# Second MoE of a chained kernel: where its second weights are split, and how a block's activations are split beside the block before

## The chip, the cores and the metric

One core of a Trainium2 chip runs the whole program in one launch. The metric is device time in microseconds (us): the kernel before took a median of 1038.61 us in 3 runs (1037.12 to 1039.48). The profile is of one further execution.

The core's engines run their own instruction queues in order and wait for each other by semaphores: TensorE (PE in the profile, its weight loads PEld) multiplies, VectorE (DVE) and GpSimd (POOL) do element-wise arithmetic, ScalarE (ACT) copies and applies functions, and SyncE (SP) issues the DMAs.

## The reference

All tensors are float; the MoE weights come as float64, and the kernel converts them to float32 itself ("wide" in the code).

```
x = attention(q, k, v, f)            # 4 x 8 heads, 576 tokens, 64 wide
x = x as 2304 tokens x 512
h = x @ moe_w_in                     # 512 -> 2048
g = h * clip(h + 3, 0, 6) / 6
x = g @ moe_w_out                    # 2048 -> 512
h = x @ moe2_w_in                    # the second MoE: 512 -> 2048
g = max(h, 0) + log1p(exp(-|h|))
out = g @ moe2_w_out                 # 2048 -> 512
```

## The kernel before, in words

The program is recorded as a list of operations, each with the engines that may do it, its planned cost, the data that it reads and writes, and a due time `at`. `Work.order` then simulates the engines and at each turn takes the operation that can start first, or, among those ready at once, the one with the smallest `at`; what comes out is one fixed order for each engine. An operation with two ways (`either`: VectorE or GpSimd) goes to the one that would end first by the planned costs, with 600 ns in GpSimd's favour (`pv`).

Every product in float32 precision is made of three matmuls on split operands: a high half (a copy in the type fp32r, made by ScalarE) and a low half (the operand less its high half, made by VectorE or GpSimd). So every weight and every activation that is multiplied needs one ScalarE copy and one subtraction.

**The first MoE** (lines 1278 to 1388) runs over five blocks of tokens, four of 512 and one of 256. The last two blocks run together, unit by unit (`NB - 2` and `NB - 1` in the code): 16 slices of the hidden width, for each of which both blocks have a first product (line 1290), the activation (lines 1330, 1332), its split (lines 1310, 1311, 1313) and a second product (line 1353). They stand at about 500 to 636 us of the span. In the same time the second MoE's first weights are loaded in float64 (line 1001), converted on VectorE and ScalarE (lines 1017 to 1023), combined (line 1100) and split (lines 1129, 1132) into the tiles that the first MoE's weights leave free.

**The second MoE** uses a Strassen scheme with 7 products in place of 8 (`SEVEN`). A unit is a pair `p` of slices, 8 units in all. For each unit four sums of the weight quarters are formed (line 1100) and seven factors split.
- *Stage A* (`step_a`, line 1406) is the first matrix with the softplus: 4 blocks `t` of 576 tokens, 8 steps `p` each, 42 matmuls a step. ScalarE copies four products of a step (line 1421), VectorE adds three (line 1424), and lines 1449, 1451 and 1452 make the softplus. The order of products in a step is `CHAIN`; the accumulators of a product that is added to can be used again only when the copy or the add is done.
- `factors_x(t)` prepares a block's activations: it loads them from x2_dram (line 1197), forms four differences (line 1212) and splits seven factors (lines 1206, 1207), into the tile XO for even blocks and MX and SB for odd ones. In the kernel before it is recorded at the start of block `t - 1`, with due times 4 us apart.
- `weights2_out(p)` prepares the second matrix of unit `p`: it loads the unit's two slices, converted earlier, from wf_dram (line 1086) into staging tiles (GT and rBL, or st), forms four sums (line 1100), splits seven factors (lines 1129, 1132) into four pairs of small buffers (`piece`) in SB, rBW, MX and PC, and stores each half to wo_dram (line 1161). In the kernel before it is recorded at every third step of stage A.
- *Stage B* (`step_b`, line 1507) is the second matrix; it loads the units back from wo_dram (line 1168) and prepares the activations of g (lines 1472 to 1490).

## Time and profile before

| | |
|---|---|
| three runs, median | 1038.61 us (1037.12 to 1039.48) |
| profiled execution, its own time | 1037.48 us |
| its span | 1035.7 us |
| TensorE busy | 985.4 us, 95% |
| VectorE, ScalarE, GpSimd busy | 835.5, 599.1, 281.7 us |
| granted TensorE clock, mean | 0.993 |
| first MoE's last blocks | about 500 to 636 us |
| stage A, blocks 0 to 3 | from 636.1, 690.9, 744.8 and 797.8 us |
| stage B | from about 843 us to the end |

Two views matter: how long each engine is busy in a stretch, and, for the engine that idles, what ended its idle time. The busy share over the whole span says little here, since the stages have different limits.

### The profile page before, as it was taken

How to read it: one execution, taken by the hardware profiler on the slowest of the kernel's cores; microseconds unless marked ns; L12 is line 12 of the kernel's file. 1: busy time of each engine (PE TensorE's matmuls, PEld its weight loads, DVE VectorE, ACT ScalarE, POOL GpSimd, SP SyncE). 2: the span in 40 equal slices, each digit the busy share in tenths (PEclk: the TensorE clock that was granted, in tenths of full speed). 3: DMA queues.
4: the chain of work that ended last, by engine and by line, in shares of the span. 5: the costliest groups of instructions: out<-in, count | busy, mean ns of one | idle time of the engine just before them, and what ended most of it. 6: DMA issues, size and time to landing. Idle time of an engine off the chain costs nothing.

```text
span 1035.7 us, 17877 instructions
## 1 busy us (share of the span) xinstructions
PE 985.4 (95%) x6116; PEld 853.1 (82%) x6116; DVE 835.5 (81%) x1653; ACT 599.1 (58%) x1309; POOL 281.7 (27%) x273
## 2 busy tenths in 40 slices
PE   8999998989999999999999999898989999999998
PEld 6666677768788888888788888797979999999997
DVE  8789979998998669986865656989796768888885
ACT  6898766877676556664443335656655544443342
POOL 2221231230000000000311211756560307454442
PEclk9999999999999999999999999999999999999999
DMA  6675553445553235412612114695963994445342
GB/s 140 161 155 141 134 148 94 119 142 147 130 153 95 59 114 149 113 43 78 195 44 65 58 41 156 203 307 197 323 228 127 344 373 157 123 124 153 113 126 77
DMA packets 192771, 151.50 MB, mean 146 GB/s; under 512 B 108988, under 2 KB 166492, under 8 KB 191784
## 3 DMA queue, kind: packets, MB, share of 16 engines
q1 hardware_dynamic: 192680, 150.36, 48.6%
q8 instruction: 48, 0.79, 0.3%
q14 instruction: 43, 0.35, 0.1%
HBM read 98.10 MB, written 52.21 MB: 145 GB/s over the span
## 4 chain that ended last, share of the span: by engine, by line
PE 63%; DVE 21%; issue 5%; DMA 4%; ACT 3%; POOL 2%; SPq 1%; DVEq 0%; ACTq 0%; POOLq 0%
PE bank L1507 15%; PE bank L1353 14%; PE bank L1290 14%; PE bank L1406 8%; PE bank L685 5%; PE bank L846 4%; PE bank L776 4%; DVE st L1020 2%; DVE st L1023 1%; DVE p L701 1%; DVE MX L1313 1%; DVE GT L1332 1%; DVE rBW L1449 1%; DVE KB L632 1%; SPq L535 1%
## 5 line engine op out<-in xcount | busy, mean ns | idle before, releaser
L1290 PE MATMUL bank<-MX,W 128*128 128x512 f32 x768 | 224.1, 405 | 1.7 <-DVE MX L886 1.0
L1353 PE MATMUL bank<-MX,W 128*128 128x512 f32 (+1 forms) x688 | 188.5, 382 | 3.7 <-DVE MX L1313 3.7
L1290 PEld LDWEIGHTS bank<-MX,W 128*128 128x128 f32 x768 | 133.6, 190 | 24.2 <-DVE MX L886 1.3
L1353 PEld LDWEIGHTS bank<-MX,W 128*128 128x128 f32 x688 | 121.3, 189 | 25.5 <-DVE MX L1313 4.3
L1507 PE MATMUL bank<-rW,rW 128*128 128x256 f32 x1134 | 138.7, 283 | 1.7 <-POOL rW L1132 0.9
L1507 PEld LDWEIGHTS bank<-rW,rW 128*128 128x128 f32 x1134 | 136.9, 191 | 2.6 <-POOL rW L1132 1.1
L1406 PE MATMUL bank<-XO,rW 128*128 128x288 f32 x672 | 97.2, 302 | 13.0 <-DVE rBW L1424 6.5
L1406 PEld LDWEIGHTS bank<-XO,rW 128*128 128x128 f32 x672 | 92.0, 191 | 17.6 <-DVE rBW L1424 8.2
L710 ACT ACTIVATE p<-p,stats 64x64 f32<-64x64 f32 (+4 forms) x130 | 72.3, 557 | 33.4 <-DVE stats L701 32.5
L1486 ACT ACTIVATE rW<-st 128x512 fp32r<-128x512 f32 (+1 forms) x72 | 36.9, 518 | 77.1 <-PE bank L1507 43.5
L1406 PE MATMUL bank<-MX,rW 128*128 128x288 f32 x480 | 71.1, 299 | 7.4 <-DVE HY L1424 4.5
L1036 POOL TENSOR_TENSOR W<-st,W 128x512 fp32r<-128x512 f32 x24 | 34.0, 1418 | 162.3 <-ACT W L1035 111.5
L1406 PEld LDWEIGHTS bank<-MX,rW 128*128 128x128 f32 x480 | 65.6, 188 | 10.0 <-DVE HY L1424 5.9
L1330 ACT ACTIVATE GT<-bank,three 128x512 f32<-128x512 f32 x80 | 51.1, 643 | 31.0 <-PE bank L1290 15.1
L581 POOL TENSOR_TENSOR V<-vr,V 128x640 fp32r<-128x640 f32 x10 | 17.1, 1715 | 189.8 <-ACT V L577 189.8
L776 PE MATMUL bank<-ident,p 128*128 128x128 f32 x390 | 58.7, 276 | 8.7 <-DVE xs L861 4.4
L776 PEld LDWEIGHTS bank<-ident,p 128*128 128x128 f32 x390 | 46.3, 141 | 24.8 <-DVE xs L861 3.9
L1313 DVE TENSOR_TENSOR MX<-GT,MX 128x512 fp32r<-128x512 f32 (+1 forms) x69 | 49.5, 720 | 21.1 <-ACT MX L1310 20.2
L811 ACT ACTIVATE pth<-bank 128x320 fp32r<-128x320 f32 (+2 forms) x100 | 42.5, 433 | 34.5 <-PE bank L776 25.7
L1490 POOL TENSOR_TENSOR rW<-st,rW 128x256 fp32r<-128x256 f32 (+1 forms) x35 | 40.9, 1173 | 73.2 <-ACT rW L1486 58.8
L701 DVE CUSTOM_DVE_ANT_0 p<-bank,bar 64x64 f32<-64x64 f32 (+4 forms) x130 | 52.1, 421 | 9.8 <-PE bank L685 9.0
L1332 DVE SCALAR_TENSOR_TENSOR GT<-GT,bank 128x512 f32<-128x512 f32 x80 | 49.9, 628 | 8.1 <-ACT GT L1330 7.5
(241 smaller groups left out, 2130.8 us busy)
## 6 DMA issues: line engine op xcount, KB each, us to landing
st<-g_dram SPq DMA_DIRECT2D x36, 512.0 KB
st<-in_moe_w_out_dram SPq DMA_DIRECT2D x32, 512.0 KB
st<-in_moe_w_in_dram SPq DMA_DIRECT2D x26, 512.0 KB
g_dram<-HY SPq DMA_DIRECT2D x16, 576.0 KB
g_dram<-rBW SPq DMA_DIRECT2D x16, 576.0 KB
rW<-wo_dram SPq DMA_DIRECT2D x5, 1792.0 KB
wo_dram<-SB SPq DMA_DIRECT2D x42, 128.0 KB
wo_dram<-rBW SPq DMA_DIRECT2D x42, 128.0 KB
```

Of the source, the lines that this page charges most:

```text
L685: nc.tensor.matmul(acc[:r, o:o + c - a], qs[:, q0:q0 + r], ks[:, a:c], start=(n == 0 and ti == todo[-1][0]), stop=(n == len(ops) - 1), ski ...
L701: nc.vector.tensor_tensor_reduce(out=T["P"][par][ti][:r, a:c], in0=bank[bk.i][:r, o:o + c - a], in1=bar[:r, b0:b0 + c - a], op0=ALU.add, o ...
L710: nc.scalar.activation(out=pt, in_=pt, func=ACTF.Exp, scale=-1.0, bias=sv[:r, 0, ti:ti + 1], accum_out=sv[:r, 1, ti:ti + 1],)
L776: nc.tensor.transpose(acc[:, p0:p0 + P], T["P"][par][ti][:, k0:k0 + P], ident)
L811: nc.scalar.activation(out=place("PTH", j, ks, a, c), in_=src(), func=ACTF.Copy)
L1290: nc.tensor.matmul(bank[bk.i][:, 0:n], w[:, c], x[:, c, 0:n], start=(c == 0 and p == 0), stop=(c == NC - 1 and p == 2))
L1313: op(("dve", dve(n), lambda: nc.vector.tensor_tensor(t(glt), g, t(ght).bitcast(F32), op=ALU.subtract)), r=[("g", i), ("gh", i3)], w=[("gl" ...
L1330: op(("act", act(n, True, 1), lambda: nc.scalar.activation(out=g, in_=bank[bk.i][:, 0:n], func=ACTF.Relu, bias=three)), r=["three"], banks ...
L1332: op(("dve", dve(n), lambda: nc.vector.scalar_tensor_tensor(out=g, in0=g, scalar=6.0, in1=bank[bk.i][:, 0:n], op0=ALU.min, op1=ALU.mult)), ...
L1353: nc.tensor.matmul(bank[b][:, o:o + n], w[:, c * P:(c + 1) * P], x, start=(ft == 0 and p == 0 and o == 0), stop=(ft == NF - 1 and p == 2), ...
L1406: nc.tensor.matmul(bank[bks[b].i][:, 0:HA], wa[u][:, c], xa[v][:, c], start=(nm in ("P1", "P2", "P5") and c == 0 and y == 0), stop=(c == 1 ...
L1507: nc.tensor.matmul(bank[bks[b].i][:, o * 256:(o + 1) * 256], ga[u], wa[v], start=(p == 0 and o == 0 and y == 0), stop=(p == NPR - 1 and y ...
```

## The change

`weights2_out` moves from stage A into the first MoE's last two blocks: it is recorded there for units 0 to 6, with due times beside those of the first weights. Its loads go to the tile XO (four slices' room, used by turns), its sums to XT, and its split factors to the rest of XO: 11 pieces, each with both halves, stored by one DMA of 256 KB where two of 128 KB stood. XO and XT are those that `factors_x(0)` fills, which now comes behind all of this. The tile PC goes.

`factors_x(t + 1)` is recorded after step 6 of block `t`, with due times 5 us apart, and each of its differences and ScalarE copies gets one more dependency ("pace"): the i-th waits for product P6 of step i of block `t`.

```diff
     def weights2(o, p, at, parts, i0):
...
+        own = i0 >= 8
+
+        def raw(i):
+            return BIG["XO"][:, (i - 8) * NC * P:(i - 7) * NC * P].bitcast(F32)
...
         for z in range(2):
             i, ft = i0 + z, 2 * p + z
-            if (o, ft) in late2:
+            if not own and (o, ft) in late2:
                 raw_weights(i, 1, o, ft, at, True)
...
             def load(i=i, ft=ft):
-                dst = words(i)[:, 0]
+                dst = raw(i) if own else words(i)[:, 0]
                 if wide:
                     nc.sync.dma_start(out=dst, in_=wf_dram[o, ft])
...
-            dma(load, 4 * P * NC * P, w=[("stage", i), ("up", i)] + [("o", i, 0), ("o", i, 1)] * (i < 2), r=["m2"] * (i in (2, 3)) + [("wf", o, ft)],
+            dma(load, 4 * P * NC * P, w=[("stage", i), ("up", i)] + [("o", i, 0), ("o", i, 1)] * (i < 2), r=["m2"] * (i in (2, 3) or own) + [("wf", o, ft)],
                 at=at - 15, name="loadwf")
...
         def x(i, e, j, n=1):
+            if own:
+                return (BIG["XT"][:, i * 2 * h:] if e else raw(i0 + i))[:, j * h:(j + n) * h]
             return words(i0 + i)[:, e, j * h:(j + n) * h]
...
-        s0, s1, u0, u1 = ((x, i0 + i) for x in ("stage", "up") for i in range(2))
+        s0, s1, u0, u1 = ((x, 8 + i if own and x == "up" else i0 + i) for x in ("stage", "up") for i in range(2))
...
-            rd = [("stage", i0 + i), ("up", i0 + i)]
+            rd = [(s0, s1)[i], (u0, u1)[i]]
...
+    NPC = (7 * XW - 4 * NC * P) // (4 * P)
+
     def piece(i):
-
-        t, a = ((BIG["SB"], 2 * XW + i * 2 * P) if i < 3 else (BIG["rBW"], 2 * XW + (i - 3) * 2 * P) if i < 6 else
-                (MX, 5 * XW) if i == 6 else (BIG["PC"], 0))
-        return t[:, a:a + 2 * P]
+        return BIG["XO"][:, 4 * NC * P + i * 4 * P:][:, 0:4 * P].rearrange("p (s f) -> p s f", s=2)
...
         for z in range(7):
-            i = pieces[0] % 4
+            i = pieces[0] % NPC
             pieces[0] += 1
...
             def store(z=z, i=i):
-                for s in range(2):
-                    dma(lambda s=s: nc.sync.dma_start(out=wo_dram[p][:, (s * 7 + z) * 2 * P:(s * 7 + z + 1) * 2 * P], in_=piece(2 * i + s).bitcast(F32)), 8 * P * P,
-                        r=[("piece", i)], w=[("wo", p, z, s)], at=at, name="storewo")
-
-            parts.append((z, z + 1, lambda s, i=i: piece(2 * i + s).bitcast(F32R), [("piece", i)], store))
+                dma(lambda: nc.sync.dma_start(out=wo_dram[p].rearrange("p (s z f) -> p s z f", s=2, z=7)[:, :, z], in_=piece(i).bitcast(F32)), 16 * P * P,
+                    r=[("piece", i)], w=[("wo", p, z)], at=at, name="storewo")
+
+            parts.append((z, z + 1, lambda s, i=i: piece(i)[:, s], [("piece", i)], store))
         weights2(1, p, at, parts, i0)
...
         dma(lambda: nc.sync.dma_start(out=unit2_w(p).rearrange("p s z f -> p (s z f)").bitcast(F32), in_=wo_dram[p]), 4 * P * UW,
-            r=[("wo", p, z, s) for z in range(7) for s in range(2)], w=[("unit2", p)], at=at, name="loadwo")
+            r=[("wo", p, z) for z in range(7)], w=[("unit2", p)], at=at, name="loadwo")
...
     def factors_x(t, at, step):
 
         z = t % 2
+
+        def pace(x):
+            return [("pace", t - 1, x)] if t else []
...
-        def split(f, src, key, at):
-            op(("act", act(n, False), lambda: nc.scalar.activation(out=xf(z, f, 0), in_=src(), func=ACTF.Copy)), r=[key], w=[("xf", z, f)], at=at, name="xfh")
+        def split(f, src, key, at, x):
+            op(("act", act(n, False), lambda: nc.scalar.activation(out=xf(z, f, 0), in_=src(), func=ACTF.Copy)), r=[key] + pace(x), w=[("xf", z, f)], at=at, name="xfh")
             op(either(n, lambda e: e.tensor_tensor(xf(z, f, 1), src(), xf(z, f, 0).bitcast(F32), op=ALU.subtract)), r=[key], w=[("xf", z, f)], at=at, name="xfl")
 
...
             key = [("xt", y) if isinstance(y, int) else ("xf", z, y) for y in (a, b)]
-            op(either(n, go), r=key + ["m2"], w=[("xt", d)], at=at + step * i, name="x" + f)
-            split(f, lambda d=d: sm(d), ("xt", d), at + step * (i + 0.5))
+            op(either(n, go), r=key + ["m2"] + pace(i), w=[("xt", d)], at=at + step * i, name="x" + f)
+            split(f, lambda d=d: sm(d), ("xt", d), at + step * (i + 0.5), i)
         for i, f in enumerate(("B11", "B21", "B22")):
-            split(f, lambda f=f: raw(f), "m2", at + step * (4 + i))
+            split(f, lambda f=f: raw(f), "m2", at + step * (4 + i), 4 + i)
...
-        for nm, n in (("XO", 7 * XW), ("SB", 2 * NC * tokens(LAST_B) + 2 * TB), ("PC", 2 * P)):
+        for nm, n in (("XO", 7 * XW), ("SB", 2 * NC * tokens(LAST_B) + 2 * TB)):
...
-            op(("pe", 6 * (0.447 * HA + 2.5), go), r=[("unit", p), ("xf", z, f)], w=[bks[b]], banks=[bks[b]], at=at, name=nm, seq="s" if nm in ("P1", "P2", "P5") else None)
+            op(("pe", 6 * (0.447 * HA + 2.5), go), r=[("unit", p), ("xf", z, f)], w=[bks[b]] + [("pace", t, p)] * (nm == "P6"), banks=[bks[b]], at=at, name=nm, seq="s" if nm in ("P1", "P2", "P5") else None)
...
     for p in range(NPR):
         freed(of_pair(p), [("unit", p)], lambda p=p: again(p, UW, F32R, ("U", p)))
         weights2_in(0, p, moe_at(NB - 2, 2 * p + 2) + 14, 2 if p in (1, 3, 5) else 0)
+        if p < NPR - 1:
+            weights2_out(p, moe_at(NB - 2, 2 * p + 1) + 14, 8 + p % 2 * 2)
         if p == NPR - 2:
...
+    freed([("stage", 8 + i) for i in range(4)] + [("piece", i) for i in range(NPC)], [("xf", 0, f) for f in AT[2]])
+    freed([("up", 8), ("up", 9)], [("xt", 0), ("xt", 1)])
     factors_x(0, M2_0 - 45, 4.0)
...
-    freed([(x, c) for x in "XY" for c in range(NC)] + [(x, i) for x in ("gh", "gl") for i in range(3)], [("xf", 1, f) for f in AT[2]] + [("piece", i) for i in range(4)])
+    freed([(x, c) for x in "XY" for c in range(NC)] + [(x, i) for x in ("gh", "gl") for i in range(3)], [("xf", 1, f) for f in AT[2]])
     for t in range(NTA):
         for p in range(NPR):
-            if p == 0 and t + 1 < NTA:
-                factors_x(t + 1, ma_at(t, 1), 4.0)
-            if p % 3 == 0 and (t * NPR + p) // 3 < NPR - 1:
-                weights2_out((t * NPR + p) // 3, ma_at(t, p, 3) + 4, 4 * (1 - (t * NPR + p) // 3 % 2))
             step_a(t, p)
+            if p == NPR - 2 and t + 1 < NTA:
+                factors_x(t + 1, ma_at(t, 1), 5.0)
             if t == NTA - 1:
                 if p < 2:
```

In the six pieces below names are the program's tiles: XO and XT as above, W and rW weights, HY and rBW the sums of stage A, st and HY staging tiles. Line numbers of the changed kernel are up to 9 higher from line 1074 on.

GpSimd at the start of the first MoE's last blocks, before: the first weights' sums (line 1100), and `factors_x(0)` (lines 1212, 1207).

```order
L1272 TENSOR_TENSOR SB<-SB 128x256 x3
L1100 TENSOR_TENSOR HY<-HY 128x256 x3
L1212 TENSOR_TENSOR XT<-XO,XT 128x576
L1207 TENSOR_TENSOR XO<-XT,XO 128x576
L1212 TENSOR_TENSOR XT<-XO,XT 128x576
L1100 TENSOR_TENSOR st_170<-st_171 128x256
L1100 TENSOR_TENSOR st_170<-st_170 128x256
```

The three rows of 576 columns are the ones that leave this place.

The same place after the change.

```order
L1281 TENSOR_TENSOR SB<-SB 128x256
L1107 TENSOR_TENSOR XT<-XO 128x256 x2
L1107 TENSOR_TENSOR XT<-XO,XT 128x256 x2
L1139 TENSOR_TENSOR XO<-XT,XO 128x256
L1139 TENSOR_TENSOR XO<-XO 128x256 x3
L1139 TENSOR_TENSOR XO<-XT,XO 128x256 x2
L1107 TENSOR_TENSOR XT<-XO,XT 128x256
L1107 TENSOR_TENSOR XT<-XO 128x256
L1107 TENSOR_TENSOR HY<-HY 128x256 x2
L1139 TENSOR_TENSOR XO<-XO 128x256 x2
L1139 TENSOR_TENSOR XO<-XT,XO 128x256
```

Behind the split of the last block's activations (line 1272, now 1281), nine rows of `weights2_out` stand where three of `factors_x(0)` stood.

VectorE in stage A, block 0, before: stage A's own lines 1424, 1449 and 1452, `factors_x(1)` (lines 1212, 1207), a weight sum (line 1100) and the last unit's first weights (line 1132).

```order
L1132 TENSOR_TENSOR rW_5665<-st_170,rW_5665 128x1024
L1424 TENSOR_TENSOR rBW<-rBW,bank_69 128x288
L1100 TENSOR_TENSOR rBL<-rBL,GT 128x256
L1449 TENSOR_SCALAR rBW<-rBW 128x2x288
L1132 TENSOR_TENSOR rW_5665<-st_171,rW_5665 128x512
L1212 TENSOR_TENSOR XT<-MX,XT 128x576
L1452 SCALAR_TENSOR_TENSOR rBW<-rBW 128x2x288
L1424 TENSOR_TENSOR rBW<-rBW,bank_69 128x288
L1132 TENSOR_TENSOR rW_5665<-st_171,rW_5665 128x256
L1207 TENSOR_TENSOR SB<-XT,SB 128x576
L1449 TENSOR_SCALAR rBW<-rBW 128x576
L1424 TENSOR_TENSOR HY<-HY,bank_72 128x288
```

Between two of line 1424 stand up to three operations that are not stage A's own.

VectorE in the same block after the change, some steps further: lines 1433, 1458 and 1461 are stage A's own, line 1216 is `factors_x(1)`.

```order
L1433 TENSOR_TENSOR HY<-HY,bank_71 128x288
L1458 TENSOR_SCALAR HY<-HY 128x576
L1461 SCALAR_TENSOR_TENSOR HY<-HY 128x2x288
L1433 TENSOR_TENSOR rBW<-rBW,bank_70 128x288
L1461 SCALAR_TENSOR_TENSOR HY<-HY 128x576
L1433 TENSOR_TENSOR rBW<-rBW,bank_72 128x288
L1458 TENSOR_SCALAR rBW<-rBW 128x2x288
L1216 TENSOR_TENSOR MX<-XT,MX 128x576
L1461 SCALAR_TENSOR_TENSOR rBW<-rBW 128x2x288
L1433 TENSOR_TENSOR rBW<-rBW,bank_72 128x288
L1458 TENSOR_SCALAR rBW<-rBW 128x576
L1216 TENSOR_TENSOR MX<-MX 128x576
```

Between two of line 1433 stands at most one factor operation; the weight sums are gone.

SP in the first MoE's last blocks, before: stores of block 2's result (line 1385), loads of the activations (line 1197) and of the first weights (line 1001).

```order
L1385 DMA x2_dram2_83<-st0_170 128x512 x2
L1385 DMA x2_dram2_83<-st1_171 128x512
L1197 DMA XO_4513<-x2_dram1_82 128x2x64
L1197 DMA XT_4516<-x2_dram1_82 128x2x64
L1001 DMA st0_170<-in_moe2_w_in_dram 128x4x256
L1385 DMA x2_dram2_83<-st1_171 128x512
L1197 DMA XT_4516<-x2_dram1_82 128x2x160
L1001 DMA st1_171<-in_moe2_w_in_dram 128x4x256
```

The loads of the first weights stand behind block 2's stores and the loads of `factors_x(0)`, which have moved back.

SP at the same place after the change (line 1394 the same stores, line 1166 the stores to wo_dram, line 1001 the first weights).

```order
L1394 DMA x2_dram2_83<-st0_170 128x512 x2
L1394 DMA x2_dram2_83<-st1_171 128x512
L1166 DMA wo_dram0_137<-XO_4513 256x1x256 x4
L1001 DMA st0_170<-in_moe2_w_in_dram 128x4x256
L1166 DMA wo_dram0_137<-XO_4513 256x1x256 x3
L1394 DMA x2_dram2_83<-st1_171 128x512
L1166 DMA wo_dram1_138<-XO_4513 256x1x256 x6
L1001 DMA st1_171<-in_moe2_w_in_dram 128x4x256
```

The loads of the first weights now stand behind stores that wait for the second weights' splits.

## Rows read from the trace of the kernel before

**Rows 1.** the page's first part: busy us (share of the span) xinstructions, by engine.

```profile
PE 985.4 (95%) x6116; PEld 853.1 (82%) x6116; DVE 835.5 (81%) x1653; ACT 599.1 (58%) x1309; POOL 281.7 (27%) x273
```

**Rows 2.** by stretch: us; PE, PEld, DVE, ACT, POOL busy (instructions); clock; DMA share; GB/s.

```profile
520.00:636.00 116.00, 116.00 (x665) 101.13 (x666) 69.11 (x122) 45.93 (x85) 19.43 (x25) 1.00 0.18 55
636.00:691.00 55.00, 47.53 (x328) 45.26 (x327) 50.58 (x76) 35.20 (x78) 34.66 (x34) 0.97 0.76 246
691.00:745.00 54.00, 47.57 (x339) 45.29 (x339) 45.96 (x75) 34.07 (x80) 30.58 (x31) 1.00 0.79 263
745.00:780.00 35.00, 30.06 (x209) 27.96 (x209) 31.45 (x49) 21.39 (x48) 20.70 (x20) 1.00 0.72 240
780.00:798.00 18.00, 17.43 (x131) 17.20 (x130) 11.58 (x23) 8.57 (x19) 0.00 (x0) 1.00 0.27 102
798.00:850.00 52.00, 50.99 (x380) 50.25 (x379) 35.10 (x65) 27.26 (x57) 8.14 (x8) 1.00 0.95 349
```

**Rows 3.** TensorE's waits, 620 to 860 us: us in total, times, longest.

```profile
PE bank L1406 <- DVE HY L1424: 9.9, 13, 1.9
PE bank L1406 <- DVE rBW L1424: 9.3, 8, 2.3
```

**Rows 4.** TensorE in order of time, stage A: start us, us, instructions; first of each block.

```profile
636.14 5.05 PE L1406 MATMUL bank<-XO,rW 128*128 128x288 f32 x36
690.95 0.96 PE L1406 MATMUL bank<-MX,rW 128*128 128x288 f32 x6
...
744.81 0.96 PE L1406 MATMUL bank<-XO,rW 128*128 128x288 f32 x6
...
780.92 17.01 PE L1406 MATMUL bank<-XO,rW 128*128 128x288 f32 x126 [0.57 <-DVE HY L1424]
797.76 0.97 PE L1406 MATMUL bank<-MX,rW 128*128 128x288 f32 x6
```

**Rows 5.** VectorE's groups by form, 636 to 690 us: busy us, mean ns, idle before.

```profile
L1452 DVE SCALAR_TENSOR_TENSOR HY<-HY 128x576 f32<-128x576 f32 x7 | 6.9, 998 | 0.3 <-ACT HY L1451 0.3
L1449 DVE TENSOR_SCALAR rBW<-rBW 128x576 uint32<-128x576 uint32 x6 | 4.9, 810 | 0.0
```

**Rows 6.** the same groups in the quiet stretch, 780 to 843 us.

```profile
L1452 DVE SCALAR_TENSOR_TENSOR HY<-HY 128x576 f32<-128x576 f32 x10 | 7.5, 754 | 4.7 <-ACT HY L1451 4.7
L1449 DVE TENSOR_SCALAR rBW<-rBW 128x576 uint32<-128x576 uint32 x10 | 4.3, 456 | 0.3
```

**Rows 7.** groups by form of three engines, 500 to 636 us.

```profile
L1207 DVE TENSOR_TENSOR XO<-XT,XO 128x576 fp32r<-128x576 f32 x3 | 2.3, 758 | 0.0
...
L1100 DVE TENSOR_TENSOR st<-st,st 128x256 f32<-128x256 f32 x4 | 1.8, 461 | 0.1
...
L1129 ACT ACTIVATE rW<-st 128x256 fp32r<-128x256 f32 x4 | 1.6, 407 | 0.0
...
L1132 POOL TENSOR_TENSOR rW<-st,rW 128x256 fp32r<-128x256 f32 x4 | 3.0, 739 | 29.3 <-ACT rW L1129 29.3
```

**Rows 8.** waits of all engines, 520 to 636 us.

```profile
ACT MX L1310 <- PE bank L1353: 28.6, 13, 5.2
...
DVE MX L1313 <- ACT MX L1310: 19.3, 13, 4.3
```

**Rows 9.** GpSimd, VectorE and TensorE in order of time, 511 to 523 us.

```profile
511.01 2.02 POOL L1212 TENSOR_TENSOR XT<-XO,XT 128x576 f32<-128x576 f32 x1 [2.68 <-DVE XO L1207]
...
511.65 1.67 DVE L1019 TENSOR_SCALAR st<-st 128x512 uint32<-128x512 uint32 x1
...
522.88 0.42 DVE L1019 TENSOR_SCALAR st<-st 128x512 uint32<-128x512 uint32 x1
...
518.03 0.50 PE L1353 MATMUL bank<-MX,W 128*128 128x512 f32 x1 [1.45 <-DVE MX L1313]
```

**Rows 10.** SP's issues of line 1161: ns min/median/max, first and last start us.

```profile
L1161 SPq DMA_DIRECT2D wo_dram<-SB x42: 319/418/1564, 654.8 to 764.6; - x42
...
L1161 SPq DMA_DIRECT2D wo_dram<-MX x14: 382/412/896, 660.8 to 771.3; - x14
```

## The prediction

> **What bounds the kernel now.** I read four views, in this order. The page's first part says that TensorE is busy 95% of the span of 1035.7 us [rows 1], so only a stretch where it idles can give much. The table by stretches shows where that is: in 520 to 636 us (the first MoE's last two blocks) TensorE is busy all 116 us, while in 636 to 691 and 691 to 745 (stage A, the second MoE's first matrix) it is busy 47.5 of 55 and 47.6 of 54 [rows 2]. The same rows name the other side: VectorE is busy 50.6 of 55 and 46.0 of 54 there, and only 69.1 of 116 in the blocks before. The list of waits confirms it: nearly all of TensorE's waiting in stage A is for line 1424, VectorE's add of a product onto the sum, 9.9 + 9.3 us [rows 3].
>
> How much stage A loses is read from TensorE's own instructions [rows 4]. The undisturbed pace stands at 780.92: 126 matmuls until 797.76, 16.84 us, 0.1337 us each. A block has 8 steps of 42 matmuls, 336, so 44.9 us (5.62 a step). Block 0 runs from 636.14 to 690.95, 54.8 us, with 324 of its matmuls (the last 12 come after the next block's first), 43.3 at the clean pace: it loses 11.5, of which the granted clock of 0.97 [rows 2] is 3% of 55, 1.7 us. Block 1 runs to 744.81, 53.9 us: 8.9 lost. Block 2 to 797.76, 52.95: 8.0 lost. Together **28.4 us**. In block 3 nothing is prepared for a later block; TensorE is busy 51.0 of 52 us there, with VectorE at 35.1 [rows 2]: about 1 us, which I leave as it is.
>
> **The change part by part.**
>
> *The second weights' splitting leaves stage A.* It is 88 two-way VectorE or GpSimd operations there: 8 units of 4 sums and 7 low halves. Before, 8 units run and not 7: the stores to wo_dram are 42 from SB, as many from rBW, 14 from MX and 14 from PC [rows 10], 112 or 8 x 14, and the order stores wo_dram2 twice. With it go 56 ScalarE copies and GpSimd's load: 34.7, 30.6 and 20.7 us in the three stretches of blocks 0 to 2 [rows 2].
>
> *What VectorE has left in blocks 0 to 2.* Its own work of a step is read where nothing else runs: 11.58 us in 18.0 us [rows 2], so 0.643 x 5.62 = 3.6 us a step, 28.9 a block. The factors of the next block are 11 operations a block, 33 for three; the changed order puts 28 on VectorE and 5 on GpSimd. At 0.76 us [rows 7] that is 8 x 0.76 = 6.1 us in block 0 and 7.6 in blocks 1 and 2. Block 0 keeps the last unit of first weights (two conversions of three operations, one sum, two low halves: some 6 us). GpSimd keeps about 8 us of work in block 0 and 4 in each other. What that costs VectorE: the same line 1449 takes 810 ns in block 0 [rows 5] against 456 in the quiet stretch, line 1452 998 against 754 [rows 6]. Of the 50.6 us in 636 to 691, undisturbed work is an estimated 39.4 (7 steps 25.3, ten factor operations 7.6, fourteen others 6.5); 11.2 over, beside 34.7 of GpSimd, are 0.32 us for a us of GpSimd work, so 2.5 us and 1.3. VectorE's sum: 28.9 + 6.1 + 6 + 2.5 = 43.5 us in block 0, of 44.9 clean; 28.9 + 7.6 + 1.3 = 37.8 in blocks 1 and 2, 84% of clean.
>
> *What TensorE then loses.* Before, 85% (46.0 of 54) went with 8.9 us lost, but the loss is not even: the waits are single ones of up to 2.3 us [rows 3], where several factor operations stand between two of line 1424 and GpSimd holds VectorE up. The new order has one factor operation between a step's parts (the order pieces on VectorE), and hardly any GpSimd work. The lower bound is the 67% row, 35.1 of 52 with 1 us lost [rows 2]; the upper bound draws a straight line through that row and the 85% one: the loss L of a block with 37.8 us of VectorE work then solves to about 5, and block 0's, with 43.5, to about 8. I take 3.5, 3.5 and, for block 0, 6, nearer to the quiet row in blocks 1 and 2 because they share its lack of GpSimd work. Lost 13 instead of 28.4: **gain 15.4** (bounds 10 and 22.6, the latter with 4 + 0.9 + 0.9).
>
> *The new waits ("pace").* Each factor operation waits for P6 of one step of the block before. Behind it on ScalarE stand the copies of P6 and later products, which can't start before P6 either; so nothing is held up that could run. I cost it at nothing; the upper bound is one product, 6 x 0.134 = 0.8 us, for each of 7 splits in 3 blocks, 17 us, if the order put older work behind.
>
> *The splitting lands in the first MoE's last blocks.* 7 units: 77 two-way operations, 25 on VectorE and 52 on GpSimd by the new order, and 49 ScalarE copies. From rows of this stretch: 25 x 0.461 = 11.5 us on VectorE, 52 x 0.739 = 38.4 us on GpSimd, 49 x 0.407 = 20 us on ScalarE [rows 7]. VectorE has 116 - 69.1 = 46.9 us idle, GpSimd 96.6, ScalarE 70 [rows 2]. That idle time is slack: ScalarE waits 28.6 us for TensorE to give back the buffers of line 1310, and VectorE 19.3 us behind it [rows 8], so both run a buffer ahead. What hides the work is this slack; what can take it away is GpSimd holding VectorE. One place shows the size: while GpSimd ran 511.01 to 513.03, VectorE's line 1019 took 1.67 us against 0.42 at 522.88; after two more such meetings TensorE waited 1.45 us [rows 9]. So a GpSimd operation of 2.02 us cost VectorE 1.25 us, 62% of its length. On 38.4 us: 0 to 24, and at block 0's rate of 0.32, 12. Then 11.5 + 12 = 23.5 of 46.9: half the slack is left, and I charge TensorE **1.5 us**, one such wait (bounds 0 and 7, the latter for 35.5 of 46.9, with five of them).
>
> The Trainium skill, "SBUF — State Buffer", section "Who interferes with whom", says that VectorE and GpSimd share one pair under an exclusive lock, so that a VectorE instruction with two SBUF inputs is blocked for the whole of a GpSimd instruction that reads SBUF. The trace agrees in kind (1.67 us for 0.42 [rows 9]); by the full rule all 38.4 us would be blocked, which is the mechanism of the second rival.
>
> *Its transfers.* 14 loads of 256 KB and 49 stores of 256 KB, 16.5 MB, in 116 us are 142 GB/s beside the 55 that run there at a share of 0.18 [rows 2]; at that rate the share comes to 0.65, no limit. On SP the first weights' loads now stand behind stores that wait for GpSimd's splits (the order piece on SP); the conversions on VectorE wait for those loads. Cost 0 to 3 us; it is in the 1.5.
>
> *The first block's factors* move to the end of the last blocks, behind the seventh unit. In the order six of line 1341 (before, 1332) follow them on VectorE, three slices of both blocks; 16 slices in the 136 us of the last blocks are 8.5 us each, so 25 us are left before stage A needs them. No cost; once these 25 us are gone, every us more delays stage A by one.
>
> **Sum.** 15.4 - 1.5 = 13.9 us off the profiled execution's 1037.5 gives 1023.6. The median of the three runs is 1.1 us higher; I say **1024 us**.
>
> **The rivals.**
> - *VectorE stays the bound in stage A.* For it: 43.5 of 44.9 us in block 0, and 85% went with 8.9 lost before. Against it: the GpSimd work that stretched it is gone. By the straight line the blocks lose 8 + 5 + 5 = 18, a gain of 10, less 3 or 4 in the last blocks: 1031.
> - *The loss moves to the last blocks, slower.* One mechanism: GpSimd's 52 operations block VectorE for their full length, 38.4 + 11.5 = 50 us on 46.9 of slack, and VectorE saturates from 520 to 636. It decides from a blocking of 92% ((46.9 - 11.5) / 38.4) on. The price is the rate of 691 to 745, 8.9 lost on 44.9: 116 x 0.198 = 23 us, against 15.4 gained: 1037.5 + 7.6, 1045. Against it: 62% is what [rows 9] show, for an operation that met VectorE's at once. It is what the Trainium skill's rule above gives where every GpSimd operation finds VectorE waiting.
> - *Stage A becomes clean.* Blocks 1 and 2 run like 798 to 850, block 0 loses 4, the last blocks nothing: 22.6 off, 1015. For it: the operations stand one by one between the adds. Against it: block 0's 43.5.
>
> **How the numbers follow.** The forecast (10 to 19 us off) 0.54, its own range 1018 to 1028; VectorE still the bound 0.20; clean 0.16; slower 0.10. The range 1013 to 1034 leaves out the slower case, the tail of the first rival and the end of the clean one, about 0.2. A measurement here tells 0.2% (2.1 us) from no change. Faster takes the forecast, the clean case and most of the first rival, 0.86; same 0.05 (0.04 from that rival's tail, 0.01 of the slower case); slower 0.09.
>
> **What would show it.** In the profile after: TensorE's waits for the add in stage A at some 9 us instead of 19; GpSimd at 8 us or less in block 0 and 35 to 45 us more in the last blocks, VectorE at 85 to 98 of their 116 us; TensorE still at 114 or more of 116 there; stage A's blocks 48 to 52 us long. The forecast is wrong if TensorE waits in the last blocks for line 1341 or 1322, if blocks 1 and 2 still take over 51 us, or if stage A starts with a wait for its first factors.

## The result, and the profile after

Over seven runs each the changed kernel took a median of 1030.3 us (1027.4 to 1033.7), the kernel before 1039.5 (1037.1 to 1046.5); the ratio is 0.9903 with a 95% interval of 0.9881 to 0.9925. The forecast was 1024, the range 1013 to 1034. So the change is faster, as forecast, and the time lies inside the range. The two terms of the sum were both wrong: stage A gained more than forecast and the last blocks lost far more.

The page's first part after, which answers to [rows 1] (busy us by engine):

```profile
PE 979.6 (95%) x6116; PEld 849.7 (83%) x6116; DVE 843.0 (82%) x1671; ACT 596.5 (58%) x1300; POOL 255.7 (25%) x246
```

It hides everything: the shares are those of before. The stretches show it. The first 500 us end at 495.4 to 501.2 us in the 14 profiles of this case, so the last blocks are measured from a marker inside each trace, the line 1341 (before, 1332) that follows VectorE's idle time of 3.39 us: 499.24 before, 496.61 after. Before, from the marker to stage A (columns as in [rows 2]):

```profile
499.24:636.14 136.90, 134.90 (x768) 116.70 (x767) 89.78 (x150) 56.77 (x106) 29.45 (x34) 1.00 0.21 66
```

After: the last blocks, a piece of them, stage A's blocks 0 to 2, and the rest.

```profile
496.61:649.55 152.94, 139.39 (x768) 118.07 (x767) 124.31 (x185) 71.78 (x153) 72.29 (x78) 0.99 0.52 167
507.00:520.00 13.00, 12.44 (x60) 10.63 (x61) 11.74 (x20) 5.47 (x13) 7.03 (x8) 0.87 0.76 241
649.50:697.70 48.20, 44.95 (x326) 43.40 (x326) 39.76 (x68) 29.21 (x58) 11.60 (x10) 1.00 0.49 160
697.70:743.00 45.30, 45.30 (x338) 44.93 (x337) 35.84 (x68) 26.40 (x55) 1.53 (x1) 1.00 0.38 132
743.00:788.90 45.90, 45.57 (x339) 45.03 (x338) 36.80 (x70) 26.34 (x55) 3.50 (x3) 1.00 0.32 117
788.90:1026.80 237.90, 229.78 (x1861) 227.63 (x1860) 184.94 (x289) 98.81 (x172) 96.99 (x88) 1.00 0.54 177
```

Blocks 0 to 2 of stage A took 161.6 us [rows 4] and take 139.3, 22.3 less. The last blocks take 152.9 instead of 136.9, 16.0 more. From block 3 to the end it is 237.9 us in both. With the marker's 2.6 us that is the 8.9 by which the spans differ (1035.7 and 1026.8); without it the change is worth 6.3 us by these rows.

TensorE's waits after, 500 to 860 us (us, times, longest), answer to [rows 3]:

```profile
PE bank L1299 <- DVE GT L1341: 12.1, 8, 3.6
PE bank L1415 <- DVE HY L1433: 2.7, 4, 1.0
PE bank L1362 <- DVE MX L1322: 1.3, 2, 0.7
PE bank L1415 <- ACT HY L1430: 1.2, 1, 1.2
PE bank L1415 <- ACT rBW L1430: 0.5, 1, 0.5
```

The waits for the add (line 1433) fell from 19.2 to 2.9 us (a last row has 0.2), and a wait for line 1341, the first MoE's activation, has come: 12.1 us. The longest of these shows how it arises. VectorE in order of time (start us, us):

```profile
501.07 1.23 DVE L1322 TENSOR_TENSOR MX<-GT,MX 128x512 fp32r<-128x512 f32 x1
502.21 0.96 DVE L1019 TENSOR_SCALAR HY<-HY 128x512 uint32<-128x512 uint32 x1
503.10 0.95 DVE L1139 TENSOR_TENSOR XO<-XT,XO 128x256 fp32r<-128x256 f32 x1
503.97 0.94 DVE L1019 TENSOR_SCALAR HY<-HY 128x512 uint32<-128x512 uint32 x1
504.83 2.34 DVE L1020 SCALAR_TENSOR_TENSOR HY<-HY 128x512 uint32<-128x512 uint32 x2
507.10 0.41 DVE L1341 SCALAR_TENSOR_TENSOR GT<-GT,bank 128x256 f32<-128x256 f32 x1
507.43 0.68 DVE L1023 SCALAR_TENSOR_TENSOR HY<-HY 128x512 uint32<-128x512 uint32 x1
```

GpSimd in the same microseconds:

```profile
500.82 0.92 POOL L1139 TENSOR_TENSOR XO<-XT,XO 128x256 fp32r<-128x256 f32 x1
501.71 2.92 POOL L1139 TENSOR_TENSOR XO<-XO 128x256 fp32r<-128x256 f32 x3
504.59 2.03 POOL L1139 TENSOR_TENSOR XO<-XT,XO 128x256 fp32r<-128x256 f32 x2
```

While GpSimd splits second weights without a pause, line 1019 takes 0.96 us against 0.42 [rows 9]; when GpSimd stops at 506.6, line 1023 has 0.68. Line 1341 itself is short (0.41): it came late because of what stood ahead of it. TensorE waited 3.65 us for it, and the granted clock of 507 to 520 is 0.87. Cut finer, that is the lower of the clock's two levels, half of the full one, in a short piece at the end of the wait, and the full clock behind it (columns as before):

```profile
507.10:510.50 3.40, 2.94 (x8) 2.48 (x9) 2.98 (x8) 1.47 (x3) 0.39 (x1) 0.50 0.93 248
510.50:520.00 9.50, 9.50 (x53) 8.16 (x52) 8.66 (x13) 4.01 (x10) 6.63 (x8) 1.00 0.69 237
```

TensorE was busy 139.4 us for the same 768 matmuls that took 134.9. So of the 16.0 us some 11.5 are idle time and 4.5 longer busy time. The piece at half clock explains at most 1.7 of the 4.5. Each stop adds a little more: three matmuls of 512 columns are busy for 0.86 us, but the next ones start 0.70 us after them when nothing is waited for, so a stop shows this overlap as busy time. For the eight waits more than before this comes to an estimated 1.3 us; the rest is open. (Number 4 below has TensorE busy 3.1 us longer than before at a granted clock of 1.00.)

### The profile page after: what moved, and what is told of

Same layout as the page of the kernel before. It is cut to its first block, busy times and chain, and to the rows that moved or that the text cites. A ratio compares the mean times of both kernels' runs of the same rounds, so it can differ in the third digit from the quotient of the medians.

```text
span 1026.8 us, 17687 instructions
## 1 busy us (share of the span) xinstructions
PE 979.6 (95%) x6116; PEld 849.7 (83%) x6116; DVE 843.0 (82%) x1671; ACT 596.5 (58%) x1300; POOL 255.7 (25%) x246
## 5 line engine op out<-in xcount | busy, mean ns | idle before, releaser
L1415 PE MATMUL bank<-XO,rW 128*128 128x288 f32 x672 | 92.8, 298 | 3.6 <-DVE HY L1433 1.7
L1495 ACT ACTIVATE rW<-st 128x512 fp32r<-128x512 f32 (+1 forms) x72 | 36.9, 518 | 76.9 <-PE bank L1516 42.9
L1322 DVE TENSOR_TENSOR MX<-GT,MX 128x512 fp32r<-128x512 f32 (+1 forms) x69 | 52.2, 759 | 8.9 <-ACT MX L1319 8.2
L1341 DVE SCALAR_TENSOR_TENSOR GT<-GT,bank 128x512 f32<-128x512 f32 x80 | 49.5, 626 | 8.4 <-ACT GT L1339 7.8
```

The source lines that it names most:

```text
L1322: op(("dve", dve(n), lambda: nc.vector.tensor_tensor(t(glt), g, t(ght).bitcast(F32), op=ALU.subtract)), r=[("g", i), ("gh", i3)], w=[("gl" ...
L1341: op(("dve", dve(n), lambda: nc.vector.scalar_tensor_tensor(out=g, in0=g, scalar=6.0, in1=bank[bk.i][:, 0:n], op0=ALU.min, op1=ALU.mult)), ...
L1415: nc.tensor.matmul(bank[bks[b].i][:, 0:HA], wa[u][:, c], xa[v][:, c], start=(nm in ("P1", "P2", "P5") and c == 0 and y == 0), stop=(c == 1 ...
```

## The experiments

All times "from the marker" are the last blocks, "A" is the sum of stage A's blocks 0 to 2; the busy times (us) are those of the table by stretches from the marker to stage A, and each ratio is to runs of the kernel before on the same chip.

| kernel | from marker | GpSimd | VectorE | A | median us, ratio to before [95%] |
|---|---|---|---|---|---|
| before | 136.9 | 29.5 | 89.8 | 161.6 | 1039.5 |
| changed | 152.9 | 72.3 | 124.3 | 139.3 | 1030.3, 0.9903 [0.9881, 0.9925] |
| 1 pacing alone | 136.9 | 29.4 | 89.8 | 158.2 | 1034.9, 0.9960 [0.9941, 0.9979] |
| 2 move alone | 153.3 | 72.4 | 124.8 | 148.6 | 1040.4, 1.0021 [1.0000, 1.0042] |
| 3 moved work on VectorE | 144.0 | 36.9 | 118.9 | 137.8 | 1023.4, 0.9857 [0.9822, 0.9892] |
| 4 moved work on GpSimd | 151.2 | 95.0 | 115.7 | 138.2 | 1028.1, 0.9906 [0.9873, 0.9939] |
| 5 transfers alone | 145.1 | 37.1 | 95.7 | 138.8 | 1021.3, one run |
| 6 move, factors on VectorE | 153.9 | 71.5 | 124.9 | 135.7 | 1028.6, one run |
| 7 GpSimd work added in A | 152.5 | 71.8 | 124.3 | 144.1 | 1033.1, one run |
| 8 all on VectorE | 134.1 | 2.1 | 118.3 | 134.7 | 1008.7, 0.9697 [0.9653, 0.9742] |
| 9 as 8, GpSimd work added | 151.0 | 36.7 | 134.7 | 134.6 | 1024.3, one run |
| 10 before, all on VectorE | 134.2 | 2.2 | 94.9 | 136.2 | 1013.6, 0.9762 [0.9732, 0.9793] |

**1 and 2: the halves of the change.** One kernel has the pacing only, the other the move only:

```
# 1: the kernel before, with the factors recorded after step 6, 5 us apart, with "pace"
# 2: the changed kernel with
-            return [("pace", t - 1, x)] if t else []
+            return []
-                factors_x(t + 1, ma_at(t, 1), 5.0)     # after step_a, p == NPR - 2
+                factors_x(t + 1, ma_at(t, 1), 4.0)     # ahead of step_a, p == 0
```

> The kernel before with one half of the change alone: the factors of the next block are paced (recorded after step 6, each waiting for P6 of a step); the second weights' splitting stays in stage A with its 8 units. Theory W, it is the second weights' leaving that clears stage A: TensorE's waits for the add stay at 14 us or more, blocks 0 to 2 take 155 us or more (161.6 before, 139.3 after the change), time 1033 to 1040 us. Rival P, the pacing clears it: waits of 6 us or less, blocks 0 to 2 at 148 us or less, and as the last blocks are untouched the time is below that of the changed kernel, 1015 to 1026 us.

> The changed kernel without the pacing: the next block's factors are recorded at the block's start again, 4 us apart; the second weights stay in the first MoE's last blocks. Theory W: blocks 0 to 2 of stage A at 145 us or less, stage A starting at 648 to 651 us as in the changed kernel, time 1029 to 1035 us. Rival P: blocks 0 to 2 at 152 us or more, time 1040 us or more, no better than the kernel before.

The pacing alone takes 3.4 us off stage A, the move alone 13.0, both 22.3. The first has the times that theory W named (A at 158.2, 1034.9 us), but not its waits. TensorE's waits in stage A's blocks 0 to 2 of number 1 (634.83 to 793.05 us):

```profile
PE bank L1410 <- DVE HY L1428: 5.9, 6, 1.9
PE bank L1410 <- ACT rBW L1425: 5.3, 7, 1.3
PE bank L1410 <- ACT HY L1425: 2.7, 3, 1.3
PE bank L1410 <- DVE rBW L1428: 0.9, 2, 0.7
```

Those for the add (line 1428 here) are 6.8 us, not 14 or more. Waits of 8.0 us for ScalarE's copies (line 1425), 0.8 us before, have come in their place; why ScalarE is late there was not looked into. The second fits neither theory in stage A (148.6). Its time, 1040.4 us, is the one of rival P: the move alone brings no gain, since the last blocks take back 16.4.

**3 and 4: which engine does the moved work.** One index chooses the way:

```
-            op(either(h, go), r=r, w=w, at=at - 2, name=name)
+            op(either(h, go)[0:1] if own else either(h, go), ...)    # 3; [1:2] in 4
-            op(either(n * h, lo), r=rd, w=w, at=at, name="w2l")
+            op(either(n * h, lo)[0:1] if own else either(n * h, lo), ...)
```

> The changed kernel with all 77 two-way operations of the moved second weights on VectorE, none on GpSimd (25 and 52 before). Theory C, what the last blocks lose (13.4 us later start of stage A) comes mostly from GpSimd stretching VectorE: the stretch of VectorE's instructions there falls from about 35 to about 13 us, which pays for 52 more operations of 0.41 to 0.46 us (some 22 us), so stage A starts at 643 to 650 us, no later than now. Rival Q, it comes from the added operations standing in VectorE's queue ahead of the first MoE's own: three times as many of them, stage A starts at 655 us or later. Rival D, it comes from the added transfers and SP's queue: no change, 649 to 650 us.

> The changed kernel with all 77 two-way operations of the moved second weights on GpSimd, none on VectorE. Theory C: GpSimd is busy some 90 us of the last blocks (69 now) and stretches VectorE by 10 us more, which eats what VectorE saves (25 operations, 11.5 us at clean length): stage A starts at 648 to 656 us. Rival Q: VectorE's queue holds none of them, stage A starts at 642 us or earlier. Rival D: no change, 649 to 650 us.

The last blocks of number 3:

```profile
500.92:644.90 143.98, 138.10 (x769) 118.28 (x768) 118.91 (x224) 74.28 (x157) 36.88 (x35) 0.99 0.55 176
```

With all 77 operations in VectorE's queue the last blocks are 8.9 us shorter than with 25, and VectorE is busy 118.9 us there instead of 124.3: 52 operations more, and less time. With none of them in its queue (4) it loses 14.3 us still. Stage A starts at 644.9 us in 3 and at 652.4 in 4, as theory C said. The 10 us of further stretch that it expected in 4 did not come: set against their undisturbed lengths (8 and 10), instruction by instruction, VectorE's operations of the last blocks are 30.7 us longer in 4 and 31.7 in the changed kernel. So the queue (Q) did not make the loss, nor did the transfers (D) make all of it.

**5: the transfers.** The sums and splits are left out, the loads and stores stay:

```
+        if own:
+            for z in range(7):
+                dma(... store raw(i0 + z % 2) to wo_dram[p], r=[("stage", i0 + z % 2)] ...)
+            return
```

> The changed kernel with the sums and splits of the moved units left out: the 14 loads stay, and the 49 stores of 256 KB store the loaded slices as they are (the output is then not the reference's). From one early instruction of the last blocks (the line 1341 after VectorE's idle time of 3.39 us, near 500 us) to the start of stage A the kernel before takes 136.9 us, the changed one 152.9, the one with all on VectorE 144.0. Theory C (GpSimd's work stretches VectorE's): without the operations this takes 136 to 139 us. Rival D (the transfers and SP's queue cost it): 146 us or more.

145.1 us lies between the two and decides nothing: rid of the operations, the planner gave GpSimd other work, two splits of 1024 columns (2.54 and 2.88 us) and five factor operations of block 0. Number 8 settles it: it has the same 14 loads and 49 stores, and loses nothing.

**6: what the pacing does.** Unpaced as in 2, but the factors of blocks 1 to 3 have only VectorE's way (`either(...)[:1 if t else 2]`).

> The unpaced kernel (second weights moved, factors recorded at the block's start 4 us apart), with the factors of blocks 1 to 3 on VectorE alone, none on GpSimd. Unpaced, blocks 0 to 2 took 148.6 us, paced 139.3. Theory O, it is the order (factors standing close together between the adds): 147 us or more. Theory G, it is the factor operations that the unpaced order gives to GpSimd (31 us of GpSimd work there against 17 paced, which stretch VectorE by 20.6 us against 10.8): 142 us or less.

Stage A takes 135.7 us, less than paced (139.3). Block 1 of 2, then of 6:

```profile
701.20:750.40 49.20, 45.90 (x338) 44.95 (x338) 37.76 (x63) 26.34 (x55) 7.79 (x5) 1.00 0.35 121
696.90:741.80 44.90, 44.90 (x338) 44.89 (x337) 35.27 (x69) 26.29 (x55) 0.00 (x0) 1.00 0.38 133
```

This is theory G. So what the pacing brought was not the order: GpSimd is busy 31.2 us of blocks 0 to 2 in 2, 16.6 in the changed kernel, 9.1 here.

**7: GpSimd work that nothing needs.**

```
+            if t == 1:
+                for k in range(6):
+                    op(("pool", pool(2 * P), lambda: nc.gpsimd.tensor_tensor(PC, PC, PC, op=ALU.add)), r=[("pace", t, p)], w=["PC"], ...)    # PC: the tile, as float
```

> The changed kernel with GpSimd work added that nothing needs: after P6 of each step of stage A's block 1 six additions on a tile of their own (128x256, in place), 48 in all, some 40 us of GpSimd time beside 45 us that run clean now (45.3 us, VectorE busy about 36). Theory C: they stretch VectorE by half of their length, about 20 us, so VectorE's 36 become more than the block has and block 1 takes 50 us or more, with waits for the add. Rival, the stretching needs shared tiles or comes from the DMAs: block 1 stays at 45 to 46 us.

The additions did not keep to the steps: a dependency that touches no data orders the plan and makes no semaphore, so they ran back to back, ten in block 0 and 38 beside block 1. The order on TensorE, VectorE, ScalarE and SP is that of the changed kernel, but for the place of one split on VectorE. Block 1:

```profile
697.40:746.90 49.50, 47.44 (x338) 45.21 (x338) 41.11 (x67) 26.87 (x55) 34.18 (x39) 1.00 0.35 121
```

It took 49.5 us against 45.3, with VectorE at 41.1 for the same work as 35.8: theory C in kind, but smaller than the 50 or more expected. VectorE is stretched by 5.3 us and not by 20, and its 41.1 us don't fill the block. TensorE loses 4.2 us all the same: it waits six times for the add, 2.0 us in all, and is busy 2.1 us longer at a granted clock of 1.00.

**8: no GpSimd in the second MoE's weights and factors.** `[:1]` behind each of the four `either(...)` of `weights2` and `factors_x`.

> The changed kernel with every two-way operation of the second MoE's weights and of the factors on VectorE, none on GpSimd, in the last blocks and in stage A. Theory C: VectorE gets about 24 more operations in the last blocks than with the second weights alone on it (some 13 us), and loses the rest of the stretch there (19.5 us): from the marker near 500 us to stage A 140 to 145 us (144.0 there), blocks 0 to 2 at 137 to 139 us, time 1018 to 1024 us. Rival Q, the queue: VectorE has no room for it, 148 us or more, time 1027 us or more.

```profile
495.38:629.50 134.12, 134.12 (x769) 116.86 (x768) 118.32 (x255) 73.17 (x157) 2.14 (x3) 1.00 0.57 185
629.50:673.90 44.40, 44.20 (x327) 43.39 (x326) 39.16 (x77) 29.68 (x59) 1.67 (x2) 1.00 0.56 189
673.90:718.90 45.00, 45.00 (x337) 44.87 (x337) 34.99 (x68) 26.82 (x55) 0.00 (x0) 1.00 0.38 133
```

Better than either theory: TensorE is busy all 134.12 us, with VectorE at 118.3, as much as in 3 (118.9), where the last blocks took 144.0 us beside 36.9 us of GpSimd.

**9: the same with GpSimd work that nothing needs.** Three additions a slice as in 7, in the last blocks; the order on TensorE, VectorE and ScalarE is that of 8.

> The kernel with all these operations on VectorE, with GpSimd work added in the last blocks that nothing needs: after each of the 16 first products of the wider block three additions on a tile of their own (128x256, in place), 48 in all, some 40 us. The order on TensorE, VectorE and ScalarE is the same as without them. Without them the last blocks take 134.1 us from the marker, with no wait of TensorE. Theory C: GpSimd's mere running stretches VectorE by 8 to 20 us, so 139 to 150 us, with waits for lines 1341 and 1322. Rival, it was the order that the planner writes when GpSimd is there: 134 to 136 us.

GpSimd runs them in one piece, and VectorE beside it (from the timeline, each in order of time):

```profile
501.14 38.17 POOL L1350 TENSOR_TENSOR PC<-PC 128x256 f32<-128x256 f32 x46
```

```profile
502.40 0.83 DVE L1019 TENSOR_SCALAR HY<-HY 128x512 uint32<-128x512 uint32 x1
503.15 0.83 DVE L1107 TENSOR_TENSOR XT<-XO 128x256 f32<-128x256 f32 x1
503.91 1.10 DVE L1020 SCALAR_TENSOR_TENSOR HY<-HY 128x512 uint32<-128x512 uint32 x1
...
507.72 0.41 DVE L1341 SCALAR_TENSOR_TENSOR GT<-GT,bank 128x256 f32<-128x256 f32 x1
```

The same instructions in number 8:

```profile
498.67 0.42 DVE L1019 TENSOR_SCALAR HY<-HY 128x512 uint32<-128x512 uint32 x1
499.01 0.41 DVE L1107 TENSOR_TENSOR XT<-XO 128x256 f32<-128x256 f32 x1
499.34 0.68 DVE L1020 SCALAR_TENSOR_TENSOR HY<-HY 128x512 uint32<-128x512 uint32 x1
...
501.48 0.41 DVE L1341 SCALAR_TENSOR_TENSOR GT<-GT,bank 128x256 f32<-128x256 f32 x1
```

From line 1019 to line 1341 5.3 us pass instead of 2.8. The last blocks of 9 and two pieces of them, then TensorE's waits in them:

```profile
498.69:649.70 151.01, 139.36 (x768) 120.16 (x767) 134.68 (x255) 73.18 (x157) 36.73 (x49) 0.97 0.51 165
498.70:539.30 40.60, 28.95 (x140) 23.85 (x139) 40.38 (x56) 14.51 (x34) 36.73 (x49) 0.90 0.52 171
539.30:560.00 20.70, 20.70 (x112) 17.86 (x110) 16.94 (x40) 9.31 (x21) 0.00 (x1) 0.94 0.44 141
```

```profile
PE bank L1299 <- DVE GT L1341: 11.7, 4, 5.1
```

In the first of these pieces, 40.6 us, VectorE never rests and TensorE waits 11.7 us, four times for line 1341, the longest 5.1; when GpSimd stops, so do the waits. 38.2 us of GpSimd work that no one needs cost 16.9 us, with all else in the same order: 11.7 us of waits and 5.2 us more TensorE busy time. VectorE is busy 16.4 us more, inside the 8 to 20 expected; the last blocks' 151.0 us are a little over the 139 to 150. This shows the cause in the last blocks. It is one run; in stage A the test of this kind is number 7.

**10: was the move needed?** The kernel before, with `[:1]` in the same four places.

> The kernel before, nothing moved and nothing paced, with the two-way operations of the second MoE's weights and factors on VectorE alone. Theory C (GpSimd beside VectorE is what costs; VectorE's own sum still bounds): from the marker near 500 us to stage A 134 to 136 us; in stage A VectorE has 28.9 us of its own, 8 of factors and some 11 of second weights a block, and 6 more in block 0, about 55, 48 and 48 us, so blocks 0 to 2 take 148 to 156 us (161.6 before) and the time is 1024 to 1033 us. Rival S: stage A's loss was GpSimd's alone and the move was not needed, blocks 0 to 2 at 142 us or less, time 1010 to 1018 us. Rival Q: VectorE's queue gets too long, 160 us or more, 1038 us or more.

My theory fell here in one point: I expected VectorE's own sum to bound stage A. The last blocks, and block 1 of stage A:

```profile
497.34:631.50 134.16, 134.16 (x769) 116.90 (x768) 94.92 (x180) 57.53 (x107) 2.15 (x3) 1.00 0.22 66
676.10:721.60 45.50, 45.34 (x339) 44.87 (x338) 44.05 (x100) 32.70 (x77) 0.00 (x0) 1.00 0.87 285
```

VectorE is busy 44.05 of 45.5 us, 97%, and TensorE 45.34. Before, with VectorE at 46.0 of 54 [rows 2], the block lost 8.9. So rival S holds: without GpSimd's operations, and in the order that the planner then writes, stage A's loss is gone (136.2 us), and 1013.6 us without any move beats the changed kernel. Unit 2 of the second weights is still split twice here, as in the kernel before, and not after the change; that costs nothing either. The move and the pacing on top (8) bring some 0.7% more (0.9697 over 0.9762); as the two intervals overlap a little, this is not settled.

**Two more versions of 8**, one with the last unit's both ways kept, one with stage B's factors and the activations' splits on VectorE too:

> The kernel with all on VectorE, but the last unit of second weights (prepared in stage A's block 3, used in stage B) with both ways again. From block 3 on the all-VectorE kernel took 241.2 us against 237.9 before. If this is the last unit's doing, 238 us again and 1004 to 1008 us; if not, 241 us and 1007 to 1011 us.

> As the kernel with all on VectorE, with stage B's factors of g and the splits of the first MoE's activations on VectorE too. Stage B has GpSimd busy 87 of 176 us and VectorE 143, TensorE loses some 6 us there. If GpSimd beside VectorE is the price there as well: 233 to 238 us from block 3 on, 1000 to 1007 us. If VectorE's sum gets too long (143 us less 10 to 20 of stretch plus some 35): TensorE waits for it, 243 us or more, 1011 us or more.

They took 1007.0 us, 0.9699 [0.9669, 0.9728], and 1005.8, 0.9681 [0.9656, 0.9705]; from block 3 on 239.0 and 234.8 us, against 241.2 in 8. The 239.0 lie between the two cases of the first expectation and decide nothing; the second had its first case right, 233 to 238. The three medians are not told apart by their intervals. The last, with hardly any GpSimd work in the second half, is the fastest version found, 3.2% below the kernel before.

## Why the prediction held, and where its steps failed

- **What bounds before: the waits right, the reason wrong.** Stage A did wait for line 1424, and I took VectorE's load for the reason ("85% went with 8.9 us lost"). Number 10 has VectorE busy a higher share of a block, 97%, and next to no loss: it was GpSimd running beside it.
- **"Lost 13 instead of 28.4: gain 15.4" was mis-sized.** The straight line through VectorE's busy shares gave 6 + 3.5 + 3.5; the blocks lose 4.9 (48.2 less 324 x 0.1337), 0.4 and 0.9, so the gain is 22.3, what the clean rival gave for stage A (22.6). Block 0 keeps 11.6 us of GpSimd work, more than the 8 forecast; with 5.2 us of it (6) or 1.7 (8) it takes 44.4.
- **"I charge TensorE 1.5 us, one such wait (bounds 0 and 7)" is the step that failed.** It went wrong twice. The stretch: VectorE is busy 34.5 us more in the last blocks, with 35 operations more there (the 25 and ten that the new plan gave it besides). Set against their undisturbed lengths (8 and 10), instruction by instruction, the operations are 31.7 us longer after and 7.0 before. So some 24.6 us are stretch, not the 12 that I took at stage A's rate of 0.32: about 62% of 38.4, the top of my bounds. And the price: I held slack of VectorE against stretch as two sums over 116 us. The waits are local: GpSimd's operations come in runs, VectorE's queue in that run doubles, and line 1341 stands at its end. TensorE's busy time then grows by 4.5 us, for which I had no term. Even the worst bound, 7, was less than half of 16.0.
- **The second rival named the place, not the mechanism.** The loss moved to the last blocks, at 16.0 us and not 23. But the rival decided only from a blocking of 92% on, with VectorE saturated. The stretch was some 62%, and VectorE was busy 124.3 of 152.9 us; single waits made the loss all the same. And 16.0 is less than the 22.3 gained, so the kernel did not get slower.
- **The row beside the Trainium skill's rule** is not the right one: line 1019 of [rows 9] has one input tile, and the sentence is on two. An operation with two was held up just behind it in the same trace: line 1313, MX from GT and MX, 128x512, took 1.90 us at 516.08, where the same on SB took 0.69 at 520.60.
- **The sum** was 13.9; the rows give 22.3 - 16.0 = 6.3 and the ratio 7.8 to 12.4. Two errors of opposite sign, a gain 6.9 too small and a loss 14.5 too small, left the time inside the range: that is luck. 1030.3 us is outside the forecast's own 1018 to 1028, and it stands at the 1031 of the first rival, whose mechanism did not come: the blocks lose 6.2 us, not 18. Why the runs show some 1.5 us or more beyond the rows is open; four profiles with these last blocks agree on them (152.5 to 153.9), so it is not their spread.
- **"The new waits": cost nothing, right, but for another reason.** A dependency of this kind made no wait in the running program (7 and 9). So the pace only changed the plan, and by number 6, one run, its gain (148.6 to 139.3 in A) came through which operations it left to GpSimd.
- **Transfers and the first factors: right.** The DMA share is 0.52 with no loss of its own (8 has 0.57), and stage A does not start with a wait for its factors.
- **What would have shown it** was named: "the forecast is wrong if TensorE waits in the last blocks for line 1341". It did. GpSimd's 43 us more there are within the 35 to 45. VectorE's busy time from 520 on, 102.4 us, is over the 85 to 98, but the stretch has grown from 116 to 130 us, and as a share (79%) it is what was forecast. TensorE, at 114 or more of 116 in the forecast, is busy 120.1 of these 130. In stage A the waits for the add are 2.9 us, not 9, and two of the blocks are shorter (45.3 and 45.8) than the 48 to 52 forecast.

## What to carry to other kernels

A planner that gives an operation to GpSimd because it "ends first" there must charge VectorE for it: here each us of GpSimd work with SBUF tiles cost VectorE 0.16 us where it was less loaded (7: 5.3 for 32.7 more), and 0.35 to 0.56 in the last blocks (4: 23.7 for 68.1 more; 9: 16.4 for 38.2; the change: 24.6 for 44.3 more, lengths of instructions added up). Beside a busy VectorE it cost 0.44 us of the last blocks' time (9: 16.9 for 38.2). So where both engines can do an operation, time the version with VectorE alone too. Judge a stretch by what stands in the queue ahead of the late instruction and at what stretched length, and not by a busy share: VectorE at 97% of a block cost TensorE 0.6 us (10), at 85% 8.9 us (before).

## What the runs showed of the hardware

- Beside GpSimd running without a pause (9, one addition each 0.83 us) most of VectorE's operations on SBUF tiles take 0.42 us longer each, whatever their size: 0.41 to 0.83, 0.68 to 1.10. A few are stretched less, none more. Operations with one input tile are stretched too (line 1019). Line 1341, with one input in SBUF and one in a PSUM bank, is not stretched (0.41 in both).
- The Trainium skill, "SBUF — State Buffer", section "Who interferes with whom", says that an operation of VectorE with at most one SBUF input, outside certain two-port modes, doesn't meet GpSimd. Line 1341 agrees with it. Line 1019, also with one, is stretched; whether it runs in such a mode no run shows. For two inputs the rows of 9 differ from the block for the full length that I weighed: 0.42 us for additions that follow each other every 0.83 us.
- The granted clock often falls to its lower level when TensorE has waited, and not always. In the changed kernel it is 0.50 from 507.1 to 510.5 us, at the end of the wait of 3.65 us and behind it. In 9 it is 0.50 from 524.6 to 528.0 and from 534.9 to 541.7, at waits of 5.07 and 2.87 us. But in 6 a wait of 3.67 us, up to 509.6, has 1.00 behind it, and so has one of 2.78 us in 4. In the last blocks of 8 and 10, where TensorE never waits, it is 1.00 throughout.
